# Attention and gated FFN on one core: the second half of the queries in four chunks of 256, and VectorE's second banks chosen by a budget

## The chip, the cores and the metric

The kernel runs on one NeuronCore of a Trainium2 chip. The metric is the device time in microseconds of one execution. Of the engines, TensorE (PE in the profile, its weight loads PEld) multiplies matrices into PSUM, ScalarE (ACT) evaluates exponentials and tanh, VectorE (DVE) does elementwise work, GpSimd (POOL) a few small operations, and SyncE (SP) issues nearly all transfers. Each engine works through its own instructions in order; an instruction that waits holds up all that stand behind it on its engine.

## What is computed

One layer in bf16: S = 2048 tokens, D = 512, H = 32 heads of 16, FFN width F = 1792. The gate is a plain sigmoid.

```python
qkv = (layernorm(x) @ wqkv).reshape(B, S, 3, H, 16)      # -> q, k, v of (B, H, S, 16)
p = softmax(einsum("bhqd,bhkd->bhqk", q, k) * 16 ** -0.5)
o = einsum("bhqk,bhkd->bhqd", p, v)                      # (B, H, S, 16)
h = x + o.transpose(0, 2, 1, 3).reshape(B, S, D) @ wo
n = layernorm(h)
out = h + (sigmoid(n @ w_gate) * (n @ w_up)) @ w_down
```

The scores are 32 x 2048 x 2048, so the kernel takes some 134 million exponentials; each row of scores has a bound subtracted beforehand (from the norms of q and k), so no maximum over scores is needed.

## The kernel before

**Chunks, units, steps.** The queries are cut into `CHUNKS` (L43): three of 512 columns and two of 256. Per chunk the 32 heads are worked in eight groups of four. A *unit* is one PSUM bank of 512 score columns: one head, one tile of 128 keys by 512 queries, or two key tiles by 256 queries (`per_bank`, L387). Three units are a *step* (`groups`, L394): their scores go to one of the two three-bank PSUM buffers `pss2`, and one ScalarE instruction (L782) takes the exponential of all three banks. There are 2048 units and so 683 steps; four steps are a *cycle* (`CYC`). 341 steps cover the first two chunks, 171 the third, 85 or 86 each of the last two.

**Second engine for exponentials.** In the steps in `split` (every fourth, L904) ScalarE takes two banks and VectorE the third, by five instructions that build the exponential from the bits of a float (`exp_bits`, `exp_first`, `exp_second`, `exp_third`, L800-L815) spread over this step and the next three. Before the change `twice` (L905-L911) marks further steps, every fourth or third cycle in fixed stretches, where another bank (a *second bank*) goes to VectorE. The first of a cycle is at step 0 of its four, the second at step 2. Their scratch lies in buffers that are free at the time (`scratch_of`, L793), for second banks in the one of the two `OT` buffers that is not in use.

**Scores.** `emit_scores` (L752) multiplies `KT` with `QB`. Heads lie so that two heads can share the array, each on 64 rows (*paired*, the shape 64*128 in the profile), or a head can use all 128 rows, half of them zero (*unpaired*, 128*128). Steps with an odd number are paired and even ones unpaired; in a cycle with a second bank all four are paired. `idle` (L756) holds when the filler has nothing for TensorE, and only in the first two steps of a cycle; such steps are unpaired in any case.

**PV and normalization.** `emit_pv` (L845) accumulates P times V (with a column of ones) over all keys in the one PSUM bank `acc`. At the end of a head group `emit_norm` (L822) copies `acc` to `xs_all` on VectorE (L826), sends the four rows of sums through DRAM to spread them, takes reciprocals (L837), sends them back as `rb_all` (L841) and scales into `OT` (L833): nine transfers on SP. The next group's queries come with four transfers of L221 and two of L231.

**Filler.** All other matmuls are put between the steps by a generator, `filler` (L730), driven by `emit_fill` (L867): projections of V, K and Q early on, then for each chunk `ffn_tasks` (L615): output projection with residual and layernorm (`ffn_wo`, or the denser `ffn_wo_tight` for the last chunks), gate and up (`ffn_up`), and down (`ffn_down`). `yield ("at", n)` means: go on at step n of a cycle. `ffn_up` gives a place to each gate block and each up block; a gate block is followed by tanh on ScalarE (L522), an up block by the multiply on VectorE (L530). A block fills one bank: one slice of 128 FFN columns by 512 queries (four matmuls), or two slices by 256 (eight). The list `(3, 1)` makes two blocks a cycle, `(3, 0, 1)` three (L582). All of filler shares one PSUM bank, "pm". An FFN starts at a step that depends on the end of its chunk's attention (L739) and after the FFN before it.

**Start and end.** The prologue (L236) makes what the first head group needs; its last V tiles are copied from PSUM to `Vaug` by ScalarE (`v_tile`, L307), between which the row with the bound is sent (`emit_q_bound`, L379, one of its two transfers issued by ScalarE). At the end `wo_early` (L626) does the last chunk's output projection of its first tile as far as it goes, and `ffn_last` (L641) the rest of the last chunk with nothing else beside it.

Of the kernel before, what the change touches and what calls it, by code (L numbers as in the profile page):

```python
# [13 lines left out]
ACT = mybir.ActivationFunctionType  # L14
AX = mybir.AxisListType


@with_exitstack
def kernel(
# [12 lines left out]
    P = 128  # L32
# [9 lines left out]
    TQ = QC // P  # L42
    CHUNKS = [(0, QC), (QC, QC), (2 * QC, QC), (3 * QC, QC // 2), (3 * QC + QC // 2, QC // 2)]  # L43
    NC = len(CHUNKS)
# [81 lines left out]
    o4 = 2 * GU * QC  # L126
    pt_late = slots(stg, 2) + [QTu[:, 0:3, 0:QC]]
    late_scratch = (stg[:, o4:o4 + 2 * QC].bitcast(mybir.dt.int32), e_man, y0[:].bitcast(FP32))
# [86 lines left out]
    def emit_q_rows(n):  # L215
        c, g = qgs[n]
        q0, w = CHUNKS[c]
        assert ("q", q0 // QC, g // 2) in ready
        for j in range(4):
            r = 64 * (g % 2) + DH * j  # L220
            nc.sync.dma_start(out=QB[n % 2][32 * j:32 * j + 32:2, j, 0:w],  # L221
                              in_=QTu[r:r + DH, g // 2, q0:q0 + w])

# [12 lines left out]
    def prologue(pro):  # L236
# [61 lines left out]
        def q_chunk():  # L298
            ps = pm_tile()
            for c in range(DC):  # L300
                qk_mm(ps, 0, 0, 0, c)
            nc.scalar.mul(out=QTu[:, 0, 0:QC], in_=ps[:], mul=QS)
            square("q", ps, QS)
            ready.add(("q", 0, 0))
            emit_q_rows(0)

        def v_tile(t):  # L307
            ps = pm_tile()
            for c in range(DC):
                v_mm(ps, t, c)  # L310
            v_store(t, ps, nc.scalar.copy)
            ready.add(("v", t))
# [133 lines left out]
    def fill_q0(b):  # L446
        ps = pm_tile()
        for c in range(DC):
            yield 1
            qk_mm(ps, 0, b, 0, c)  # L450
        q_store(QTu[:, b, 0:QC], ps)
        sq = squares(QTu[:, b, 0:QC])
        yield ("gap", 2)
        pn = pm_tile()
        yield 1
        norm_mm(pn, b, sq[:])
        q_root(pn, 0)
        q_bound(0, True)
        ready.add(("q", 0, b))
        ready.add(("b", 0, b))  # L460
        yield ("gap", 1)

    def fill_q(qc):
        cols = slice(qc * QC, (qc + 1) * QC)
        sq4 = stages[qc % 2]
        for b in range(4):
            ps = pm_tile()
            for c in range(DC):
                yield 1
                qk_mm(ps, 0, b, qc, c)  # L470
            q_store(QTu[:, b, cols], ps)
            nc.vector.tensor_tensor(out=sq4[:, b * QC:(b + 1) * QC], in0=QTu[:, b, cols], in1=QTu[:, b, cols],
                                    op=ALU.mult)
# [12 lines left out]

    def tiles_of(c):
        q0, w = CHUNKS[c]
        return range(q0 // P, (q0 + w) // P)

    def wo_mm(ps, c, tt, g):
        assert ("o", c, g) in ready
        nc.tensor.matmul(ps[:], lhsT=OT[c % 2][:, g, tt * P:(tt + 1) * P], rhs=wo_pad[:, g, :],  # L493
                         start=(g == 0), stop=(g == NG - 1))
# [129 lines left out]
    early = {}  # L624

    def wo_early(c):  # L626
# [14 lines left out]
    def ffn_last(c):  # L641
# [30 lines left out]
        nc.vector.tensor_tensor(out=OT[c % 2][:, NG - 1, 0:w], in0=xs, in1=rb[:, 0:w], op=ALU.mult)  # L672
        ready.add(("o", c, NG - 1))
        wo(1, 5, NG - 1)
        add_x(1)
# [54 lines left out]
    def filler():  # L730
# [91 lines left out]
    def emit_norm(c, g, i):  # L822
        w = CHUNKS[c][1]
        b = w // 32
        xs, rb, s32, r32 = (norm_part(t, w, g) for t in (xs_all, rb_all, s32_all, r32_all))
        nc.vector.tensor_copy(out=xs, in_=acc[:, 0:w])  # L826
        sd = dram.tile([4, w], FP32, name="sd", tag="sd%d" % w)
# [4 lines left out]
        def scale():  # L832
            nc.vector.tensor_tensor(out=OT[c % 2][:, g, 0:w], in0=xs, in1=rb, op=ALU.mult)  # L833
            ready.add(("o", c, g))
# [162 lines left out]
```

## Time and profile before

| | |
|---|---|
| median of 3 runs | 967.2 us (965.63 to 968.48) |
| profiled execution, its own time | 967.36 us |
| its span, first to last instruction | 965.6 us |
| first exponential starts, last one ends | 35.26, 934.89 us |
| granted TensorE clock, mean | 0.995 |
| transfers | 37500 packets, 28.38 MB |

The costliest groups of the page (instruction, tiles and shape, count, then busy time and mean of one, then the engine's idle time before them with what ended most of it):

```
L771 PE MATMUL pss<-QB,KT 64*128 64x512 bf16 (+3 forms) x2545 | 473.1, 338 | 86.8 <-ACT pt L782 40.5
L782 ACT ACTIVATE pt<-pss 128x1536 bf16<-128x1536 f32 (+1 forms) x392 | 500.6, 1361 | 18.0 <-PE pss L771 14.6
L801 DVE TENSOR_SCALAR stg<-pss 128x512 int32<-128x512 f32 x123 | 84.8, 690 | 73.0 <-PE pss L771 61.1
L852 PE MATMUL acc<-pt,Vaug 128*17 128x512 bf16 (+1 forms) x1471 | 114.1, 342 | 5.3 <-DVE xs_all L826 3.7
L533 PE MATMUL pm<-wd,reg 128*128 128x512 bf16 x173 | 51.5, 384 | 5.7 <-issue 3.2
```

The mean duration of a matmul is longer than its share of time, since matmuls overlap in the array. The exponentials appear in several groups, by the buffer that they write (pt, stg, wd, QTu); their counts add up to the 683 steps, so the n-th of them in time is step n, and a stage of the program can be placed in the trace by its steps.

### The profile page before, as it was taken

The numbers are of one execution on the slowest core, as the hardware profiler recorded it, in microseconds if no ns is written. First come the engines' busy times: TensorE is split into PE (matmuls) and PEld (weight loads), VectorE is DVE, ScalarE is ACT, GpSimd is POOL, SyncE is SP. The second block draws the span as 40 slices with busy tenths as digits, with TensorE's granted clock in tenths as the row PEclk, the third lists the DMA queues.
The fourth block names the chain that finished last, engine by engine and source line by source line (L and its number), as shares of the span: only waits on it lengthen the run. The fifth ranks groups of instructions, "written<-read, shape, count | busy, mean of one in ns | idle before, by whom it ended". The sixth has DMA issues, their size and how long they took to land.

```text
span 965.6 us, 17138 instructions
## 1 busy us (share of the span) xinstructions
PE 829.0 (86%) x6324; PEld 335.3 (35%) x6422; DVE 789.6 (82%) x1424; ACT 896.7 (93%) x769; POOL 39.0 (4%) x45
## 2 busy tenths in 40 slices
PE   4888888888888899888778999988788999998998
PEld 2221222222223232222223233222255545555646
DVE  8489999888878988898888888888899688777653
ACT  4799999999999999999999999989998999999872
POOL 4600000000000000000000000000000000000000
PEclk9999999999999999999999999999999999999999
DMA  5002341000013000000000000001011000110010
GB/s 161 20 1 56 114 95 38 15 15 3 15 25 104 15 15 16 9 19 27 15 26 27 16 16 15 9 20 26 16 26 27 16 10 16 27 32 16 9 35 12
DMA packets 37500, 28.38 MB, mean 29 GB/s; under 512 B 17708, under 2 KB 32776, under 8 KB 37416
## 3 DMA queue, kind: packets, MB, share of 16 engines
q1 hardware_dynamic: 35828, 25.71, 10.1%
q10 hardware_dynamic: 1588, 1.58, 0.5%
q8 instruction: 50, 0.82, 0.4%
q14 instruction: 34, 0.28, 0.1%
HBM read 20.31 MB, written 2.61 MB: 24 GB/s over the span
## 4 chain that ended last, share of the span: by engine, by line
PE 41%; DVE 26%; ACT 24%; issue 6%; DMA 2%; SPq 0%; ACTq 0%; DVEq 0%; POOL 0%; POOLq 0%
PE pss L771 20%; ACT pt L782 13%; PE acc L852 8%; PE pm L517 6%; ACT stg L782 4%; ACT wd L782 4%; DVE stg L801 3%; PE pm L533 2%; ACT QTu L782 2%; DVE st L137 2%; DVE reg L804 2%; PE pm L493 2%; DVE pt L814 2%; DVE y L810 1%; DVE reg L530 1%
## 5 line engine op out<-in xcount | busy, mean ns | idle before, releaser
L771 PE MATMUL pss<-QB,KT 64*128 64x512 bf16 (+3 forms) x2545 | 473.1, 338 | 86.8 <-ACT pt L782 40.5
L782 ACT ACTIVATE pt<-pss 128x1536 bf16<-128x1536 f32 (+1 forms) x392 | 500.6, 1361 | 18.0 <-PE pss L771 14.6
L771 PEld LDWEIGHTS <-KT 64*128 64x128 bf16 (+1 forms) x2560 | 179.0, 95 | 346.2 <-issue 237.4
L782 ACT ACTIVATE stg<-pss 128x1536 bf16<-128x1536 f32 (+1 forms) x140 | 183.3, 1358 | 5.0 <-PE pss L771 4.2
L801 DVE TENSOR_SCALAR stg<-pss 128x512 int32<-128x512 f32 x123 | 84.8, 690 | 73.0 <-PE pss L771 61.1
L852 PE MATMUL acc<-pt,Vaug 128*17 128x512 bf16 (+1 forms) x1471 | 114.1, 342 | 5.3 <-DVE xs_all L826 3.7
L782 ACT ACTIVATE wd<-pss 128x1536 bf16<-128x1536 f32 (+1 forms) x80 | 103.8, 1393 | 1.4 <-PE pss L771 1.3
L782 ACT ACTIVATE QTu<-pss 128x1024 bf16<-128x1024 f32 (+1 forms) x71 | 95.6, 1347 | 1.7 <-PE pss L771 1.2
L807 DVE SCALAR_TENSOR_TENSOR y<-reg 128x512 f32<-128x512 f32 x123 | 85.2, 693 | 4.2
L810 DVE SCALAR_TENSOR_TENSOR y<-y,reg 128x512 f32<-128x512 f32 x123 | 84.3, 685 | 1.1
L852 PEld LDWEIGHTS <-Vaug 128*17 128x17 bf16 x2560 | 50.5, 89 | 97.8 <-issue 83.2
L517 PE MATMUL pm<-reg,reg 128*128 128x512 bf16 (+1 forms) x252 | 55.6, 333 | 8.6 <-DVE reg L530 6.5
L517 PE MATMUL pm<-reg,wu 128*128 128x512 bf16 (+1 forms) x280 | 58.1, 338 | 1.5 <-ACT sg L522 1.2
L533 PE MATMUL pm<-wd,reg 128*128 128x512 bf16 x173 | 51.5, 384 | 5.7 <-issue 3.2
L804 DVE TENSOR_SCALAR reg<-stg 128x512 int32<-128x512 int32 x123 | 52.1, 423 | 2.0
L144 POOL TENSOR_TENSOR rs<-ve,pw_neg 128x1 f32<-128x1 f32 (+1 forms) x24 | 16.4, 685 | 896.0 <-DVE ve L142 895.8
L852 PE MATMUL acc<-stg,Vaug 128*17 128x256 bf16 (+1 forms) x564 | 50.7, 326 | 0.8 <-DVE stg L814 0.4
L530 DVE SCALAR_TENSOR_TENSOR reg<-sg,pm 128x512 bf16<-128x512 f32 x56 | 38.3, 683 | 14.5 <-PE pm L517 13.9
L814 DVE SCALAR_TENSOR_TENSOR pt<-y,stg 128x512 bf16<-128x512 f32 x70 | 47.9, 684 | 1.8
L522 ACT ACTIVATE sg<-pm 128x512 f32<-128x512 f32 x56 | 35.6, 636 | 10.0 <-PE pm L517 9.6
L801 DVE TENSOR_SCALAR wd<-pss 128x512 int32<-128x512 f32 x45 | 30.9, 687 | 14.0 <-PE pss L771 13.7
L163 PE MATMUL pm<-reg 128*128 128x512 bf16 x108 | 34.4, 391 | 2.9 <-issue 1.4
(121 smaller groups left out, 712.8 us busy)
## 6 DMA issues: line engine op xcount, KB each, us to landing
rb_all<-rd SPq DMA_DIRECT2D x96, 64.0 KB
reg<-in_A_x_dram SPq DMA_DIRECT2D x8, 256.0 KB
xr<-in_A_x_dram SPq DMA_DIRECT2D x16, 128.0 KB
out_dram<-ob SPq DMA_DIRECT2D x15, 128.0 KB
rb_all<-rd SPq DMA_DIRECT2D x60, 32.0 KB
KT<-stg SPq DMA_DIRECT2D x7, 256.0 KB
reg<-in_B_w_gate_dram SPq DMA_DIRECT2D x4, 448.0 KB
wu<-in_B_w_up_dram SPq DMA_DIRECT2D x4, 448.0 KB
```

Source lines behind the costliest of these rows:

```text
L517: nc.tensor.matmul(ps[:, i * w:(i + 1) * w], lhsT=wt[:, c, f * P:(f + 1) * P], rhs=hnT[:, c, 0:w], start=(c == 0), stop=(c == DC - 1))
L522: nc.scalar.activation(out=sg[:], in_=ps[:], func=ACT.Tanh, scale=0.5)
L530: nc.vector.scalar_tensor_tensor(out=out, in0=a, scalar=1.0, in1=b, op0=ALU.add, op1=ALU.mult)
L533: nc.tensor.matmul(ps[:], lhsT=hT[:, f, tt * P:(tt + 1) * P], rhs=wd[:, f, :], start=(f == 0), stop=(f == FC - 1))
L771: nc.tensor.matmul(pss[:, ui, h * w:(h + 1) * w], lhsT=KT[rows, g, kt * P:(kt + 1) * P], rhs=QB[n_qg % 2][rows, j, 0:w], start=True, stop= ...
L782: ex = nc.scalar.activation(out=pt[:, 0:na, :], in_=pss[:, 0:na, :], func=ACT.Exp, scale=DH ** -0.5 / QS)
L801: return nc.vector.tensor_scalar(out=e_bits, in0=src, scalar1=ONE_BITS, scalar2=0.0, op0=ALU.add, op1=ALU.max)
L804: nc.vector.tensor_scalar(out=e_man, in0=e_bits, scalar1=0x7FFFFF, scalar2=-0x40800000, op0=ALU.bitwise_and, op1=ALU.bitwise_or)
L807: nc.vector.scalar_tensor_tensor(out=e_pol, in0=m, scalar=PA, in1=m, op0=ALU.add, op1=ALU.mult)
L810: nc.vector.scalar_tensor_tensor(out=e_pol, in0=e_pol, scalar=PB, in1=e_man.bitcast(FP32), op0=ALU.add, op1=ALU.mult)
L814: nc.vector.scalar_tensor_tensor(out=dst, in0=e_pol, scalar=PC, in1=e_bits.bitcast(FP32), op0=ALU.add, op1=ALU.mult)
L852: nc.tensor.matmul(acc[32 * j:32 * j + VW, 0:w], lhsT=Vaug[:, kt, 4 * g + j, :], rhs=p[:, h * w:(h + 1) * w], start=(kt == 0), stop=(kt == ...
```

## The change

- `CHUNKS`: two chunks of 512 and four of 256. The third and fourth chunk cover together what the third did; there are six chunks, so eight more head groups.
- `ffn_up`: the places are `(3, 1)` for every chunk. The denser projection and down, and the earlier start of an FFN, go by the width of the chunk instead of its place from the end, so they hold for all chunks of 256.
- Second banks: in place of fixed lists, `plan_twice` runs at the start of each cycle from step 222 to 671. It adds to an account what VectorE has to spare in a cycle of the present phase of the filler (negative in the projection), and when the account is above 2.6 it draws 3.0 and marks this cycle. It marks 26 second banks in place of 23.
- Scratch of second banks: in `OT[0]` and the second 512 queries' part of `QTu`, whose layout changes so that 512 queries lie together. `OT` of a 256-wide chunk uses the first half of its buffer (`o_part`). The first group of the first 256-wide chunk puts its copy of `acc` in a part of `QTu`.
- `idle` holds for all steps of a cycle, so all its scores are unpaired. The two buffers of `pss2` change places.
- Start: the bound's row is sent before V tile 5 instead of tile 4, and V tiles 5 and 6 are copied by VectorE.
- End: the residual of the last chunk's first tile is added (an identity matmul) in `ffn_last` instead of `wo_early`, one projection matmul of its second tile moves ahead of the reciprocals' matmul, and `wo_early` goes on as soon as each head group is there.

```diff
-    CHUNKS = [(0, QC), (QC, QC), (2 * QC, QC), (3 * QC, QC // 2), (3 * QC + QC // 2, QC // 2)]
+    CHUNKS = [(0, QC), (QC, QC)] + [(q, QC // 2) for q in range(2 * QC, S, QC // 2)]
...
-    QTu = const.tile([P, 4, S], BF16)
+    QTu = const.tile([P, NQC, 4, QC], BF16)
...
         for t in range(3, NV0):
-            if t == 4:
+            if t == 5:
                 emit_q_bound(0, (nc.sync, nc.scalar))
-            v_tile(t)
+            v_tile(t, nc.scalar.copy if t < 5 else nc.vector.tensor_copy)
...
+    def o_part(c, g):
+        w = CHUNKS[c][1]
+        return OT[c % 2][:].rearrange("p g q -> p (g q)")[:, g * w:(g + 1) * w]
...
     def ffn_up(c):
         w = CHUNKS[c][1]
-        at = cycle((3, 1) if c + 2 < NC else (3, 0, 1))
+        at = cycle((3, 1))
...
     def ffn_tasks(c):
-        tight = c + 3 >= NC
+        tight = per_bank(c) > 1
         yield ("rate", 8.0)
+        phase[0] = "wo"
         yield from (ffn_wo_tight if tight else ffn_wo)(c)
+        phase[0] = "up"
         yield from ffn_up(c)
+        phase[0] = "down"
         yield from ffn_down(c, tight)
+        phase[0] = ""
...
         for g in range(NG - 1):
-            if g == NG - 2:
-                yield 1
-                nc.tensor.matmul(early[0][:], lhsT=ident_bf[:], rhs=early["x"][0][:], start=False, stop=False)
-                yield ("from", NS - 4)
+            while ("o", c, g) not in ready:
+                yield ("gap", 0)
             yield 1
             wo_mm(early[0], c, 0, g)
...
-        wo(1, 2, 5)
+        wo(1, 2, 6)
...
-        wo(1, 5, NG - 1)
+        wo(1, 6, NG - 1)
+        add_x(0)
         add_x(1)
...
-            yield ("from", int(first_step(c + 1)) + (11 if c + 3 >= NC else 15))
+            yield ("from", int(first_step(c + 1)) + (11 if per_bank(c) > 1 else 15))
...
     def emit_scores(i):
+        if i % CYC == 0:
+            plan_twice(i)
...
-        pss = pss2[i % 2]
-        idle = i >= 3 * FIRST and i % CYC < 2 and (state["done"] or state["wait"] > i + CYC)
+        pss = pss2[(i + 1) % 2]
+        idle = i >= 3 * FIRST and (state["done"] or state["wait"] > i + CYC)
...
         if i % CYC:
-            flat = OT[(int((i - 20) / SPC) + 1) % 2][:].rearrange("p g q -> p (g q)")
-            return (flat[:, 0:2 * QC].bitcast(mybir.dt.int32), flat[:, 2 * QC:4 * QC].bitcast(mybir.dt.int32),
-                    flat[:, 4 * QC:6 * QC].bitcast(FP32))
+            flat = OT[0][:].rearrange("p g q -> p (g q)")
+            q1 = QTu[:, 1].rearrange("p b q -> p (b q)")
+            parts = [flat[:, 0:2 * QC]] if i < 2 * SPC else [q1[:, 0:2 * QC]]
+            parts += [flat[:, 4 * QC:6 * QC], flat[:, 6 * QC:8 * QC]]
+            return tuple(t.bitcast(dt) for t, dt in zip(parts, (INT, INT, FP32)))
...
+        if g == 0 and c and CHUNKS[c - 1][1] > w:
+            xs = QTu[:, 0, 3, :].bitcast(FP32)
...
     split = set(range(8, G1, CYC))
     twice = set()
-    for qc in range(1, NQC):
-        n0 = int(qc * SPC) + 52
-        for n in range(n0, min(int((qc + 1) * SPC) + 16, int(first_step(NC - 1)) + 14)):
-            if n % ((4 if n < n0 + 56 else 3) * CYC) == 0:
-                twice.add(n + 2)
-    split |= twice
+    room = {"us": 0.0}
+
+    def plan_twice(n):
+        if n < int(SPC) + 52 or n >= G1 - 8:
+            return
+        free = {"wo": -0.8, "up": 0.9, "down": 0.85}.get(phase[0], 1.05)
+        room["us"] = max(0.0, room["us"] + free)
+        if room["us"] > 2.6:
+            room["us"] -= 2.6 + 0.4
+            twice.add(n + 2)
+            split.add(n + 2)
```

More of the change, by code (lines that the diff above doesn't have):

```diff
@@ L15 @@
 AX = mybir.AxisListType
+INT = mybir.dt.int32
 @with_exitstack
@@ L126 @@
     o4 = 2 * GU * QC
-    pt_late = slots(stg, 2) + [QTu[:, 0:3, 0:QC]]
+    pt_late = slots(stg, 2) + [QTu[:, 0, 0:3, :]]
     late_scratch = (stg[:, o4:o4 + 2 * QC].bitcast(mybir.dt.int32), e_man, y0[:].bitcast(FP32))
@@ L221, in emit_q_rows @@
             nc.sync.dma_start(out=QB[n % 2][32 * j:32 * j + 32:2, j, 0:w],
-                              in_=QTu[r:r + DH, g // 2, q0:q0 + w])
+                              in_=QTu[r:r + DH, q0 // QC, g // 2, q0 % QC:q0 % QC + w])
     def emit_q_bound(n, engs=(nc.sync, nc.sync)):
@@ L301, in q_chunk @@
                 qk_mm(ps, 0, 0, 0, c)
-            nc.scalar.mul(out=QTu[:, 0, 0:QC], in_=ps[:], mul=QS)
+            nc.scalar.mul(out=QTu[:, 0, 0, :], in_=ps[:], mul=QS)
             square("q", ps, QS)
@@ L305, in q_chunk, with v_tile @@
             emit_q_rows(0)
-        def v_tile(t):
+        def v_tile(t, copy=nc.scalar.copy):
             ps = pm_tile()
@@ L310, in v_tile @@
                 v_mm(ps, t, c)
-            v_store(t, ps, nc.scalar.copy)
+            v_store(t, ps, copy)
             ready.add(("v", t))
@@ L450, in fill_q0 @@
             qk_mm(ps, 0, b, 0, c)
-        q_store(QTu[:, b, 0:QC], ps)
-        sq = squares(QTu[:, b, 0:QC])
+        q_store(QTu[:, 0, b, :], ps)
+        sq = squares(QTu[:, 0, b, :])
         yield ("gap", 2)
@@ L463, in fill_q @@
     def fill_q(qc):
-        cols = slice(qc * QC, (qc + 1) * QC)
         sq4 = stages[qc % 2]
@@ L470, in fill_q @@
                 qk_mm(ps, 0, b, qc, c)
-            q_store(QTu[:, b, cols], ps)
-            nc.vector.tensor_tensor(out=sq4[:, b * QC:(b + 1) * QC], in0=QTu[:, b, cols], in1=QTu[:, b, cols],
+            q_store(QTu[:, qc, b, :], ps)
+            nc.vector.tensor_tensor(out=sq4[:, b * QC:(b + 1) * QC], in0=QTu[:, qc, b, :], in1=QTu[:, qc, b, :],
                                     op=ALU.mult)
@@ L489, in tiles_of @@
         return range(q0 // P, (q0 + w) // P)
+    def o_part(c, g):
+        w = CHUNKS[c][1]
+        return OT[c % 2][:].rearrange("p g q -> p (g q)")[:, g * w:(g + 1) * w]
     def wo_mm(ps, c, tt, g):
         assert ("o", c, g) in ready
-        nc.tensor.matmul(ps[:], lhsT=OT[c % 2][:, g, tt * P:(tt + 1) * P], rhs=wo_pad[:, g, :],
+        nc.tensor.matmul(ps[:], lhsT=o_part(c, g)[:, tt * P:(tt + 1) * P], rhs=wo_pad[:, g, :],
                          start=(g == 0), stop=(g == NG - 1))
@@ L624 @@
     early = {}
+    phase = [""]
     def wo_early(c):
@@ L671, in ffn_last @@
                              rhs=ident_f[:], start=True, stop=True)
-        nc.vector.tensor_tensor(out=OT[c % 2][:, NG - 1, 0:w], in0=xs, in1=rb[:, 0:w], op=ALU.mult)
+        nc.vector.tensor_tensor(out=o_part(c, NG - 1), in0=xs, in1=rb[:, 0:w], op=ALU.mult)
         ready.add(("o", c, NG - 1))
-        wo(1, 5, NG - 1)
+        wo(1, 6, NG - 1)
+        add_x(0)
         add_x(1)
@@ L832, in scale @@
         def scale():
-            nc.vector.tensor_tensor(out=OT[c % 2][:, g, 0:w], in0=xs, in1=rb, op=ALU.mult)
+            nc.vector.tensor_tensor(out=o_part(c, g), in0=xs, in1=rb, op=ALU.mult)
             ready.add(("o", c, g))
```

## The prediction

> **What bounds the kernel now.** I read the busy shares first, then the busy time by stretch, then the order of time inside three stretches.
>
> ```profile
> PE 829.0 (86%) x6324; PEld 335.3 (35%) x6422; DVE 789.6 (82%) x1424; ACT 896.7 (93%) x769; POOL 39.0 (4%) x45
> ...
> ACT  4799999999999999999999999989998999999872
> ```
>
> ScalarE is the busiest engine, nearly full from the third slice on, with dents from slice 27. Its work is the exponentials of line 782; their 683 instructions are the steps of the program. How long ScalarE needs for a step is read from starts, because its records overlap:
>
> ```profile
> 452.47 3.72 ACT L782 ACTIVATE pt<-pss 128x1536 bf16<-128x1536 f32 x3
> 456.03 2.42 ACT L782 ACTIVATE stg<-pss 128x1024 bf16<-128x1024 f32 x2
> 458.28 1.09 ACT L782 ACTIVATE QTu<-pss 128x1024 bf16<-128x1024 f32 x1
> ...
> 881.24 0.59 ACT L522 ACTIVATE sg<-pm 128x512 f32<-128x512 f32 x1
> 881.71 1.03 ACT L782 ACTIVATE stg<-pss 128x1024 bf16<-128x1024 f32 x1
> ```
>
> A three-bank step starts 1.330 us before the next (median over the trace), a two-bank one, whose third bank VectorE takes, 0.924, a tanh 0.477 (881.24 to 881.71). A cycle of four steps with one two-bank step thus needs 3 x 1.330 + 0.924 = 4.914 us of ScalarE, 0.406 less with a "second bank", 0.477 more with a tanh. What a stretch takes beyond that is **lost**. First exponential 35.26, last ends 934.89; after it 30.7 us of tail. The second half:
>
> ```profile
> 711.60:740.40 28.80, 24.92 (x280) 15.03 (x284) 25.65 (x54) 25.69 (x22) 2.35 (x4) 1.00 0.11 26
> 740.40:816.70 76.30, 71.31 (x774) 40.13 (x788) 61.13 (x110) 75.83 (x71) 0.00 (x0) 1.00 0.07 16
> 816.70:855.00 38.30, 35.70 (x389) 20.06 (x392) 29.25 (x54) 35.66 (x30) 0.00 (x0) 1.00 0.09 22
> ...
> 881.70:909.00 27.30, 24.99 (x288) 18.13 (x288) 18.02 (x32) 24.05 (x24) 0.00 (x0) 1.00 0.06 14
> 909.00:934.90 25.90, 23.67 (x271) 13.98 (x276) 16.02 (x30) 24.30 (x20) 0.00 (x0) 1.00 0.12 33
> ```
>
> (Columns: window, its length, busy PE, weight loads, VectorE, ScalarE.) Lost time, cycle by cycle, in us: steps 492-523 without FFN 1.3; output projection of the third chunk's four tiles (711.6-740.4) 4.2; its gate/up, two blocks a cycle, 1.7 in 14 cycles; its four down tiles 4.3; a gap 0.1; the fourth chunk's two projection tiles 1.4; its gate/up, three blocks a cycle (876-909), 5.0; its two down tiles 2.5. Sum 20.5. The largest rate is that of the three blocks:
>
> ```profile
> 881.88 1.03 PE L517 MATMUL pm<-reg,wu 128*128 128x256 bf16 x8 [0.45 <-ACT sg L522]
> ...
> 882.84 0.61 PE L771 MATMUL pss<-QB,KT 64*128 64x256 bf16 x6
> ...
> 883.55 1.45 ACT L782 ACTIVATE stg<-pss 128x1536 bf16<-128x1536 f32 x1 [0.81 <-PE pss L771]
> ...
> 884.05 1.03 PE L517 MATMUL pm<-reg,reg 128*128 128x256 bf16 x8 [0.60 <-DVE reg L530]
> ```
>
> There is one "pm" bank. TensorE, in order, waits until tanh or the multiply has emptied it, the scores behind wait too, and ScalarE idles 0.81 us.
>
> **The change, part by part.**
>
> *Three blocks become two.* All three FFNs of width 256 run gate/up as seven cycles. Two blocks a cycle cost 1.7 / 14 = 0.12 lost a cycle at 740-817. At half width a block is eight matmuls in 1.03-1.05 us; four full-width ones take 0.98 by the same timeline. So PE gains 2 x 0.07 on its 5.05 busy of 5.37: still below ScalarE. 21 cycles x 0.12 = 2.5, against 1.7 + 5.0.
>
> *Projection.* Three pairs of tiles at 1.4 = 4.2, against 4.2 + 1.4: a row of four tiles lets VectorE's backlog grow, a pair does not. *Down.* The six tiles remain; 6.6, against 4.3 + 2.5. *Idle steps* 492-523 are filled, since the third chunk is now done earlier: 0.3 with all gaps, against 1.4. Together 13.6 against 20.5: **-6.9**.
>
> *Second banks.* The budget, run through the program, chooses 26 in place of 23; from step 492 on 9 instead of 6, at 522, 538, 550, 582, 598, 610, 642, 658, 670. Each takes 0.406 from ScalarE and puts 690 + 423 + 693 + 685 + 684 ns = 3.17 us on VectorE. The trace gives the price: in gate/up at full width, cycles holding one lost 0.09 on the mean (plain ones -0.01) and the cycles behind them 0.39; in down 0.04 and 0.66. The next bank waits for VectorE, its score bank stays occupied, PE and then ScalarE wait. So one is worth nothing in an FFN. Three more: -1.2. The three in gate/up are in the 0.12 already; of six in down one is in the rate, five add about 0.64: +3.2. **+2.0**. Bounds: repaid in full -3.7 (9 x 0.406), or +6 if each also delays the emptying of pm:
>
> ```profile
> 838.10 0.68 DVE L538 SCALAR_TENSOR_TENSOR ob<-pm,reg 128x512 bf16<-128x512 f32 x1
> 838.84 0.81 PE L533 MATMUL pm<-wd,reg 128*128 128x512 bf16 x3 [0.99 <-DVE ob L538]
> ```
>
> *Chunk of 512 as two of 256.* Units, steps and exponentials stay (683). Scores and PV get 512 more matmuls each at half the columns: start to start 109 ns against 216, and the turn from one kind to the next costs 205 against 312, the same 96 more. There are eight more head-group ends, each with a copy of acc (422 ns), a reciprocal and a scale (416) on VectorE: 2.08 us for two against 1.62, +0.46 x 8 = 3.7 us, hidden under ScalarE where VectorE has room (16-18 of 20 us busy from 475 to 697). And 16 more transfers an end on SP (128 in all), which has them at this density from 697 us on and makes VectorE wait there only 2.6 (once, at the end) and 4.3 us (twice). What is not hidden: PV waits for the copy of acc, and the scores behind it. Seven such ends fall under the second chunk's FFN (steps 342-492); by cycles with and without one, 0 to 0.4 lost each, and 0.7 at worst in a projection. I take 0.15: **+1.0** (0 to +5).
>
> [...]
>
> *Unpaired scores in all idle steps.* Unpaired, three scores take 0.86 us, and behind a short step ScalarE waits 0.15-0.16 for them (1.08 in place of 0.92 at 458.28). Now the step behind a second bank waits too: two of them, **+0.3**.
>
> *Start.*
>
> ```profile
> 31.39 1.46 ACTq L231 DMA_DIRECT2D QB<-bnd  x1
> ...
> 32.89 1.57 ACT L210 CAST Vaug<-pm 128x512 bf16<-128x512 f32 x3 [2.36 <-PE pm L158]
> ...
> 34.55 1.02 PE L771 MATMUL pss<-QB,KT 64*128 64x512 bf16 x6 [2.06 <-ACT Vaug L210]
> ...
> 35.26 5.48 ACT L782 ACTIVATE pt<-pss 128x1536 bf16<-128x1536 f32 x4 [0.81 <-PE pss L771]
> ```
>
> ScalarE issues a transfer for 1.46 us with three V copies behind it; the first scores wait for the last copy. Now V tile 4 is copied before that issue and tiles 5 and 6 by VectorE (0.69 each, idle 5.27 us there). The first scores then need the bound's row, landed at 33.35 by the semaphore records, and the copy of tile 6, some 33.3: start 33.5, **-1.0** (0 to -1.2). ScalarE being full behind it, the shift reaches the end. The swapped order of the two score buffers costs nothing.
>
> *End.* The identity matmul of tile 0 moves from before the last PV (which waited up to 0.4 behind it and three projections) into the shadow of VectorE's scale; one more projection stands before the reciprocal's matmul (+0.1): **-0.1** (±0.4). Renamed layouts of QTu and OT and the new scratch cost nothing; they lie in storage whose readers are done.
>
> Sum: -6.9 + 2.0 + 1.0 + 0.3 - 1.0 - 0.1 = -4.7. The profiled execution took 967.36 (span 965.6 and 1.8 around it), 0.2 over the median of 967.2: 962.7 there, **962.5** against the median.
>
> **Rivals.** (a) *Given back.* Second banks in down cost +6 in place of +2, or the boundaries 4 in place of 1: 966.5 or 965.5. For it: pm and acc have one buffer each; against: the cycles of 697-817 hold as many ends and lose little. (b) *VectorE becomes the bound, slower.* The one mechanism is late emptying of acc and pm: a second bank (3.17 us) ahead of a copy in its queue. The worst cycle of that kind (838.84 above; ScalarE idle 1.15) lost 1.4. Six second banks in down at 1.4 instead of 0.64 add 4.6, seven ends at 0.7 instead of 0.15 add 3.9: 971. It decides once a late emptying costs more than some 1.1 us on the mean. Against: the measured mean is half that. (c) *More.* The five second banks in down lose nothing, because PE, which sets the pace there (5.1 of 5.3 us busy a cycle), pairs its scores in those cycles and is 0.23 us shorter: 3.2 less, 959.3. (d) *The budget does nothing:* three second banks neither way; inside the range of the forecast.
>
> **How the numbers follow.** Forecast 0.60 with its own range 959.5-965.5, (a) 0.16, (b) 0.11, (c) 0.13; (d) is within the first. 0.3% is 2.9 us, about what a measurement of this kernel tells from no change: faster means below 964.3. Of the forecast 0.49 lies below it and 0.11 above: faster 0.62, same 0.27, slower 0.11. Range 957.5 to 968: it holds all but (b). The range also has room for the clock: the granted TensorE clock falls to a half for 3.4 us three times (82, 266 and 649 us), in cycles that lost 1.4, 1.4 and 2.8; one such time more or fewer moves the sum by that.
>
> **What would show it.** First exponential near 34.2; no gate/up cycle above 6 us after 870; projection stretches in pairs losing under 2 us each; last exponential near 930; tail still 30.6. Wrong if cycles of the third and fourth chunk lose more than 0.3 on the mean in gate/up, if PE waits over some 8 us in all for the copies out of acc and pm, or if the first exponential has not moved.

## The result, and the profile after

The changed kernel is slower: 969.0 us (median of 16, 965.8 to 971.2) against 964.7 (16, 963.3 to 968.5), ratio 1.0038, 95% interval 1.0027 to 1.0050. The forecast was -4.7, which made 962.5 of the 967.2 that the kernel before had shown by then; measured is +4.3, which would make 971.5 of it, above the range of 957.5 to 968. Below, a "ratio" is always to the kernel before, run on the same chip, with its 95% interval in brackets, and "lost" is the time of a four-step cycle beyond what ScalarE needs, as in the prediction. In three of the experiments one execution took 1951 to 4309 us, and it is left out of the median.

The two profiled executions are nearly equal (967.21 after, 967.36 before; the first is at the low end of its kernel's runs), so their traces are compared for places, not for the sum. The busy shares of the changed kernel and ScalarE's row of slices:

```profile
PE 826.5 (86%) x7463; PEld 393.0 (41%) x7558; DVE 799.6 (83%) x1465; ACT 894.1 (93%) x767; POOL 38.9 (4%) x45
...
ACT  4799999999999999999999999999999899899972
```

VectorE has 10 us more and ScalarE 2.6 less; of the 2.6, the three additional second banks make 3 x 0.406 = 1.2. In ScalarE's row the dent of the three-block cycles is gone, and there are two at other places, 748 to 772 and 821 to 845 us. The start and the last FFN's gate/up by the timeline:

```profile
31.37 1.46 ACTq L232 DMA_DIRECT2D QB<-bnd  x1
...
33.47 1.02 PE L781 MATMUL pss<-QB,KT 64*128 64x512 bf16 x6 [0.99 <-DMA QB<-bnd]
...
34.23 1.45 ACT L792 ACTIVATE pt<-pss 128x1536 bf16<-128x1536 f32 x1 [2.86 <-PE pss L781]
...
882.14 0.59 ACT L526 ACTIVATE sg<-pm 128x512 f32<-128x512 f32 x1
882.62 5.20 ACT L792 ACTIVATE pt<-pss 128x1024 bf16<-128x1024 f32 x4
888.06 0.60 ACT L526 ACTIVATE sg<-pm 128x512 f32<-128x512 f32 x1 [0.24 <-PE pm L521]
```

The first exponential is at 34.23 in place of 35.26, and the scores now wait for the bound's row. From this tanh to the next is one cycle, 5.9 us with a wait of 0.24. It is the slowest of this gate/up (by its steps, 644 to 647, it took 6.16 us and lost 0.77); the others lost at most 0.22. Three stages by window (length, then busy PE, weight loads, VectorE, ScalarE):

```profile
754.00:780.00 26.00, 20.41 (x238) 12.52 (x238) 22.51 (x45) 23.56 (x20) 1.17 (x2) 1.00 0.12 30
780.00:834.00 54.00, 50.67 (x610) 33.09 (x613) 44.42 (x82) 52.16 (x47) 0.00 (x0) 1.00 0.06 16
...
860.00:900.00 40.00, 37.40 (x458) 25.63 (x458) 32.91 (x61) 39.61 (x38) 0.00 (x0) 1.00 0.07 15
```

Gate/up at 256 columns (the last two rows) runs at ScalarE's pace. Around a projection (first row) ScalarE idles 2.4 of 26 us, and VectorE is busy 22.5. Eleven cycles after step 341 lost more than 1 us. Eight of them come right behind a cycle with a second bank; the other three (from steps 504, 620 and 664) lose as much in the version without late second banks. The worst, the cycle from step 524, lost 1.93 us:

```profile
718.01 0.42 DVE L847 TENSOR_TENSOR OT<-xs_all,rb_all 128x256 bf16<-128x256 f32 x1
...
718.34 0.69 DVE L822 SCALAR_TENSOR_TENSOR OT<-OT 128x512 f32<-128x512 f32 x1
...
719.06 0.69 DVE L826 SCALAR_TENSOR_TENSOR stg<-OT,QTu 128x512 bf16<-128x512 f32 x1
...
720.73 0.68 DVE L534 SCALAR_TENSOR_TENSOR reg<-sg,pm 128x512 bf16<-128x512 f32 x1
721.33 0.41 DVE L840 COPY xs_all<-acc 128x256 f32<-128x256 f32 x1
...
721.80 0.40 PE L866 MATMUL acc<-stg,Vaug 128*17 128x256 bf16 x8 [1.74 <-DVE xs_all L840]
...
723.21 0.60 ACT L526 ACTIVATE sg<-pm 128x512 f32<-128x512 f32 x1 [1.36 <-PE pm L521]
```

The second bank was at step 522, four steps ahead of the end of a head group at 526. Its last two parts (718.34 and 719.06, which read `OT`, its scratch), the scale of an earlier group (718.01), the third bank's first parts and the FFN's multiply (720.73) all stand ahead of the copy of `acc` in VectorE's queue. PV of the next group waits 1.74 us for the copy, the gate block behind it is late, and ScalarE, in order, idles 1.36 us in tanh. In all, from 475 to 936 us (engine, what it waited for: sum, times, longest), after and then before:

```profile
PEld L781 <- DVE stg L813: 16.3, 26, 2.6
...
PE pss L781 <- DVE stg L813: 8.8, 9, 2.3
PE acc L866 <- DVE xs_all L840: 8.4, 12, 1.7
```

```profile
PEld L771 <- DVE stg L801: 13.4, 24, 1.3
...
PE pss L771 <- DVE stg L801: 3.5, 7, 0.8
...
PE acc L852 <- DVE xs_all L826: 2.5, 5, 1.0
```

TensorE waits three times as long for VectorE's copy out of `acc`, and two and a half times as long for the third bank's first part to release a score buffer.

### The profile page after: what moved, and what is told of

It reads as the page before. It is cut to its first block, busy times and chain, and to the rows that moved or that the text cites. A ratio compares the mean times of both kernels' runs of the same rounds, so it can differ in the third digit from the quotient of the medians.

```text
span 965.4 us, 19652 instructions
## 1 busy us (share of the span) xinstructions
PE 826.5 (86%) x7463; PEld 393.0 (41%) x7558; DVE 799.6 (83%) x1465; ACT 894.1 (93%) x767; POOL 38.9 (4%) x45
## 4 chain that ended last, share of the span: by engine, by line
PE 40%; DVE 28%; ACT 21%; issue 7%; DMA 2%; SPq 1%; DVEq 0%; ACTq 0%; POOL 0%; POOLq 0%
PE pss L781 20%; ACT pt L792 12%; PE acc L866 7%; PE pm L521 6%; ACT wd L792 4%; ACT stg L792 4%; DVE stg L813 3%; PE pm L537 2%; DVE pt L826 2%; DVE reg L816 2%; ACT QTu L792 2%; DVE st L138 2%; PE pm L497 2%; DVE y L822 2%; DVE OT L822 1%
## 5 line engine op out<-in xcount | busy, mean ns | idle before, releaser
L781 PE MATMUL pss<-QB,KT 64*128 64x256 bf16 (+3 forms) x3065 | 472.7, 309 | 84.5 <-ACT pt L792 38.6
L781 PEld LDWEIGHTS <-KT 64*128 64x128 bf16 (+1 forms) x3072 | 214.9, 95 | 317.9 <-issue 213.7
L866 PE MATMUL acc<-pt,Vaug 128*17 128x256 bf16 (+1 forms) x1762 | 113.2, 310 | 9.5 <-DVE xs_all L840 7.7
L866 PEld LDWEIGHTS <-Vaug 128*17 128x17 bf16 x3072 | 62.4, 89 | 90.7 <-issue 78.9
L521 PE MATMUL pm<-reg,reg 128*128 128x256 bf16 (+1 forms) x315 | 56.2, 305 | 5.7 <-DVE reg L534 4.0
L521 PE MATMUL pm<-reg,wu 128*128 128x256 bf16 (+1 forms) x336 | 58.3, 310 | 0.0
L526 ACT ACTIVATE sg<-pm 128x512 f32<-128x512 f32 x56 | 35.7, 638 | 11.3 <-PE pm L521 11.3
L521 PEld LDWEIGHTS <-reg 128*128 128x128 bf16 x336 | 29.3, 98 | 26.3 <-issue 17.0
```

The costliest lines, as they stand in the source:

```text
L521: nc.tensor.matmul(ps[:, i * w:(i + 1) * w], lhsT=wt[:, c, f * P:(f + 1) * P], rhs=hnT[:, c, 0:w], start=(c == 0), stop=(c == DC - 1))
L526: nc.scalar.activation(out=sg[:], in_=ps[:], func=ACT.Tanh, scale=0.5)
L781: nc.tensor.matmul(pss[:, ui, h * w:(h + 1) * w], lhsT=KT[rows, g, kt * P:(kt + 1) * P], rhs=QB[n_qg % 2][rows, j, 0:w], start=True, stop= ...
L866: nc.tensor.matmul(acc[32 * j:32 * j + VW, 0:w], lhsT=Vaug[:, kt, 4 * g + j, :], rhs=p[:, h * w:(h + 1) * w], start=(kt == 0), stop=(kt == ...
```

## The experiments

Times are medians in us.

**No second banks late** (in the changed kernel, none after step 341; 18 go, 8 stay).

```diff
-        if n < int(SPC) + 52 or n >= G1 - 8:
+        if n < int(SPC) + 52 or n >= 2 * int(SPC):
```

> The changed kernel without the second banks from step 341 on (18 of its 26 go; 8 stay). Theory V (VectorE is late: its second banks, the denser head-group ends and the waits for the sums' transfers meet in one in-order queue, so a second bank is not repaid): time at most 1 us above the changed kernel's 969.0 and perhaps up to 3 below, although ScalarE has 18 x 0.406 = 7.3 us more to do. Rival P (second banks are repaid, the loss is the chunks' own): 973 to 976.

956.9, ratio 0.9919 [0.9901, 0.9936]. The 18 second banks, which take 18 x 0.406 = 7.3 us from ScalarE, make the kernel some 12 us slower, four times what theory V allowed for. TensorE's waits for the copy out of `acc` (from 475 to 936 us) fall from 8.4 us in 12 times to 2.8 in 4. This version beats both kernels.

**The chunks with the old list** (changed kernel, but the old fixed list of 23 second banks, old idle rule, start and buffer order) and **the other way round** (old chunks with the budget, 24 second banks, and all small edits), which has the same lines with the signs changed.

```diff
-        if i % CYC == 0:
-            plan_twice(i)
...
+    for qc in range(1, NQC):
+        n0 = int(qc * SPC) + 52
+        for n in range(n0, min(int((qc + 1) * SPC) + 16, int(first_step(NC - 1)) + 14)):
+            if n % ((4 if n < n0 + 56 else 3) * CYC) == 0:
+                twice.add(n + 2)
+    split |= twice
```

> The changed kernel with the old fixed list of second banks (23), the old idle rule, the old start and the old order of the score buffers: the four chunks of 256 and two blocks a cycle alone (with the end that they need). Theory C (the chunks cost what the change costs: head-group ends and their transfers): 967 to 970. Rival B (the budget's placing, six in down, costs it): 960 to 964.

966.9, 1.0013 [0.9998, 1.0028]: with the old list the 256-wide chunks are still 10.0 above the version without late second banks, of which about 1 is for the small edits that it lacks (they are measured alone below).

> The kernel before with all of the change but the chunks: budget (24 second banks, up to step 611 as its scratch allows), idle rule, start, end, order of buffers. Theory C: 963 to 965, the start's 1 us less than before and a little back for the idle rule. Rival B: 966 to 970.

969.5, 1.0048 [1.0032, 1.0063]: the budget slows the old chunks too. The first of the two speaks for theory C, the second for rival B: with late second banks in place, each half of the change costs.

**The old idle rule** in the changed kernel.

```diff
-        idle = i >= 3 * FIRST and (state["done"] or state["wait"] > i + CYC)
+        idle = i >= 3 * FIRST and i % CYC < 2 and (state["done"] or state["wait"] > i + CYC)
```

> The changed kernel with the old idle rule (only the first two steps of a cycle unpaired). If the unpaired scores cost what cycles 328 to 347 show (some 0.2 us for each of five cycles): 0.5 to 1.3 below the changed kernel, 968. If half-clock times of TensorE follow from less paired work, their number falls or rises with it: the clock beside the times then differs from the changed kernel's.

970.4, 1.0054 [1.0038, 1.0071], against 1.0038 [1.0027, 1.0050] for the changed kernel: unpairing all idle steps costs nothing here; the direction is the opposite of what was forecast, but the intervals overlap.

**Where a second bank stands.** In the changed kernel, the same 12 head groups of twelve steps after step 398 get one second bank each: four steps ahead of the next group's end (the list below), four behind the last end (each late number 4 less), or on it (8 less). The eight early ones stay.

```diff
-            plan_twice(i)
...
+    twice |= set([234, 250, 262, 274, 290, 302, 318, 330, 406, 426, 438, 458, 470, 490, 522, 534, 586, 598, 650, 662])
```

> The changed kernel with 12 second banks after step 341 in place of the budget's 18, each four steps ahead of a 256-wide head-group end (the end's copy out of acc comes in the step behind the second bank's last part). Against the version without any second bank after step 341 (956.9) they take 12 x 0.406 = 4.9 us from ScalarE. Theory E (a second bank costs where its four VectorE instructions stand in front of the copy of acc of a head-group end): this is the worst place, 964 to 969. Rival L (the price is VectorE's load, wherever the bank stands): the same as the two other placements, all three within 1.5 us, near 956.9 + 12/18 of 12.1 = 965. Rival N (no price away from the budget's own places): near 952 to 955.

971.4, 1.0062 [1.0041, 1.0083].

> The same 12 head groups, each second bank four steps behind an end in place of four ahead of the next (in a head group of 12 steps). Theory E: the parts are done before the next copy of acc, so most of the 4.9 us stays: 953 to 958, at least 5 below the placement ahead of the ends. Rival L: the same as that one within 1.5 us.

961.9, 0.9964 [0.9946, 0.9983].

> The same 12 head groups, each second bank in the step of the end that opens them (eight steps earlier than ahead of the next end). Theory E: between the other two, 956 to 964, because the first part (690 ns) and the last two of the third bank before it stand ahead of the copy of acc but the rest behind. Rival L: as the others within 1.5 us.

959.1, 0.9930 [0.9912, 0.9949]. The same number of second banks differs by 12 us by place alone: rival L falls, and so does rival N. Theory E has the sign, but not all of the order: ahead is worse than its 964 to 969, behind is worse than its 953 to 958, and on the end, inside its 956 to 964, is best. By the traces, the cycles that hold the 12 ends behind the list's banks (steps 410 to 666) lose 1.64 us on the mean with the banks ahead, 0.20 behind, 0.35 on and 0.23 without any late bank; VectorE is busy 5.73, 4.30, 4.51 and 4.09 us in them, where ScalarE needs 4.91 (5.39 with a tanh). With the banks behind, the cycle ahead of the end's loses 0.82 instead. Taken over a bank's own cycle and the next, and against the same cycles without late banks, a second bank makes ScalarE lose 1.51 us ahead of an end, 0.77 behind it and 0.75 on it, where it saves 0.406. TensorE's wait for the copy, banks ahead and then on the ends:

```profile
PE acc L864 <- DVE xs_all L838: 18.1, 16, 1.8
...
DVE r_all L849 <- DMA s_all<-sd: 15.2, 9, 2.5
```

```profile
DVE r_all L849 <- DMA s_all<-sd: 5.8, 5, 2.3
...
PE acc L864 <- DVE xs_all L838: 4.1, 9, 1.0
```

Two lines differ, TensorE's wait for the copy and VectorE's wait, in its reciprocal, for the denominators. Even in the best place the 12 banks gain nothing against the 956.9 without them.

**No second bank at all.**

```diff
-        if i % CYC == 0:
-            plan_twice(i)
```

> The changed kernel without any second bank: the eight of the first half (steps 234 to 330, 512-wide head groups, no FFN beside them) go too. If those are worth what ScalarE saves (8 x 0.406 = 3.2): 960.2, against 956.9 with them. If they cost what the late ones cost on the mean (12.1 / 18 = 0.67 each): 951.5.

959.1, 0.9930 [0.9909, 0.9952]; with the eight early ones it was 0.9919 [0.9901, 0.9936]. By their profiled runs the eight lose 2.6 of the 3.2 us that they take from ScalarE (steps 200 to 340: 5.8 lost against 3.2). So they are worth about nothing, and cost nothing.

**The reciprocal later**, with the banks ahead of the ends and without late banks.

```diff
-            later(i + 10, scale)
-        later(i + 5, recip)
+            later(i + 10 + 2 * slow, scale)
+        slow = c >= 2 and c < NC - 1 and g < NG - 1
+        later(i + 5 + 2 * slow, recip)
```

> The version with 12 second banks ahead of the head-group ends (971.4), with the reciprocal two steps later behind the end (i + 7 in place of i + 5) and the scale at i + 12, for the 256-wide chunks but for the last chunk and each chunk's last head group. Theory D: what costs is that VectorE, in order, stands in the reciprocal waiting for the denominators' transfers (15.2 us in 9 waits there), with the third bank's parts behind it: 961 to 965. Rival K: what costs is the late copy out of acc itself (TensorE waits 18.1 us in 16 times for it): 968 to 973, and TensorE's waits for that copy stay near 18.

970.6, 1.0053 [1.0032, 1.0074]: theory D falls; VectorE's wait in the reciprocal is down to 2.3 us in 2 times, and the time has not moved. It isn't what K expected either: TensorE's waits for the copy are 12.9 us in 14 times, not near 18. The loss has moved: the cycles of the 12 ends lose 1.02 in place of 1.64, the ones ahead of them 0.71 in place of 0.26.

> The version without second banks after step 341 (956.9) with the same later reciprocal and scale. If VectorE's waits for the denominators (13.5 us in 10 times in its profiled run) reach the end in part: 953 to 956. If they are hidden under ScalarE: 956 to 958.

961.8, 0.9965 [0.9953, 0.9978], outside both expectations. The wait went to the scale, which now has only three steps for the second round of transfers; at 666 us:

```profile
665.79 0.43 DVE L847 TENSOR_TENSOR OT<-xs_all,rb_all 128x256 bf16<-128x256 f32 x1 [4.60 <-DMA rb_all<-rd]
...
669.87 1.45 ACT L792 ACTIVATE pt<-pss 128x1536 bf16<-128x1536 f32 x1 [2.99 <-PE pss L781]
```

So the comparison of the two with the later reciprocal is not clean; what it shows is that this edit mends nothing.

**Before without its late second banks** and **the small edits alone**, both on the kernel before.

```diff
-            if n % ((4 if n < n0 + 56 else 3) * CYC) == 0:
+            if n % ((4 if n < n0 + 56 else 3) * CYC) == 0 and n + 2 < int(2 * SPC):
```

> The kernel before, without its 14 second banks after step 341. Theory E has fewer head-group ends there (24 in place of 32 after step 341) and the fixed list meets them less often, but the price is of the same kind: 957 to 962, so that the kernel before paid for its second banks too. Rival: the price came with the 256-wide ends alone; then the 14 were worth 14 x 0.406 = 5.7 and it is 968 to 971.

966.7, 1.0016 [1.0001, 1.0030], between the two expectations: before, 14 late second banks were worth 2.0 (0.1 to 2.9 by the interval) of the 5.7 us that they take from ScalarE.

The small edits (with the change's edits at the end):

```diff
-        pss = pss2[i % 2]
-        idle = i >= 3 * FIRST and i % CYC < 2 and (state["done"] or state["wait"] > i + CYC)
+        pss = pss2[(i + 1) % 2]
+        idle = i >= 3 * FIRST and (state["done"] or state["wait"] > i + CYC)
...
-            if t == 4:
+            if t == 5:
                 emit_q_bound(0, (nc.sync, nc.scalar))
-            v_tile(t)
+            v_tile(t, nc.scalar.copy if t < 5 else nc.vector.tensor_copy)
```

> The kernel before with the small edits alone: V copies and the bound's issue at the start, unpaired scores in all idle steps, the order of the two score buffers, and the end. The old fixed list of second banks and the old chunks stay. As predicted for these parts (-1.0 + 0.3 - 0.1 = -0.8): 962.5 to 965, and then the budget is what made the version without the chunk change 5 us slower. Rival: the small edits cost: 967 to 970.

963.6, 0.9990 [0.9977, 1.0003]: -1.1, where -0.8 was forecast; the interval still holds no change. Against it the version without the chunk change, which has the budget besides, is 5.8 slower: the budget's places cost that much even between the wider head groups.

**Acc in two halves**: groups of 256 columns alternate between the halves of the one bank.

```diff
+    def acc_part(c, g):
+        w = CHUNKS[c][1]
+        o = w * (g % 2) if w < QC else 0
+        return acc[:, o:o + w]
-        nc.vector.tensor_copy(out=xs, in_=acc[:, 0:w])
+        nc.vector.tensor_copy(out=xs, in_=acc_part(c, g))
...
-                nc.tensor.matmul(acc[32 * j:32 * j + VW, 0:w], lhsT=Vaug[:, kt, 4 * g + j, :],
+                nc.tensor.matmul(acc_part(c, g)[32 * j:32 * j + VW, :], lhsT=Vaug[:, kt, 4 * g + j, :],
```

> The changed kernel, with the sums of P V of a 256-wide head group in alternate halves of the acc bank, so that the next group's first matmuls need not wait for VectorE's copy of the last one. Theory K (the late copy out of acc holds TensorE, the scores behind it and ScalarE): most of the price of the 18 second banks goes, TensorE's waits for that copy fall from 8.4 us to under 2, and the time falls from 969.0 to 954 to 962. Rival Q (the price is VectorE's queue itself: the next third bank's first part comes late, which keeps its score bank, whoever holds acc): 965 to 969, the waits for score banks and for pm stay.

970.6, 1.0065 [1.0050, 1.0080].

> The version with 12 second banks ahead of the head-group ends (971.4), with the same alternate halves. Theory K: 954 to 961, below the 959.1 of the banks on the ends. Rival Q: 966 to 971.

971.5, 1.0077 [1.0065, 1.0089].

> The version without second banks after step 341 (956.9), with the same alternate halves. Its waits of TensorE for the copy are 2.8 us in 4 times: 955 to 957 by both theories; below the other two if second banks are worth nothing even then (rival Q), above them by up to 4 if they are worth what ScalarE saves (theory K).

957.2, 0.9929 [0.9915, 0.9943]. The first two are just above rival Q's numbers, but they do not speak against K, since the wait is still there (banks ahead, two halves):

```profile
PE acc L869 <- DVE xs_all L843: 17.4, 15, 1.7
```

The program still makes TensorE's write to the bank wait for VectorE's read of it, whichever half: 17.4 us in 15 times, where it was 18.1 in 16 without the halves. No run here tried the halves without that wait.

**The copy by ScalarE at the 12 ends**, with the banks ahead of them and, as control, without late banks.

```diff
+    BY_ACT = [410, 430, 442, 462, 474, 494, 526, 538, 590, 602, 654, 666]
-        nc.vector.tensor_copy(out=xs, in_=acc[:, 0:w])
+        (nc.scalar.copy if i in BY_ACT else nc.vector.tensor_copy)(out=xs, in_=acc[:, 0:w])
```

> The version with 12 second banks ahead of the head-group ends (971.4), where ScalarE in place of VectorE copies acc at those 12 ends (ScalarE isn't late, so TensorE's wait for the copy goes; it costs ScalarE some 0.45 us each by VectorE's 0.42 for the copy, 5.4 in all). Theory K (the late copy): at most 3 above the same edit without second banks (its own control, expected near 962), so 957 to 965. Rival Q (VectorE's queue itself, the next third bank's first part): 8 us or more above the control, 970 to 976.

966.0, 1.0010 [0.9998, 1.0021].

> The control: the version without second banks after step 341 (956.9) with the same 12 copies by ScalarE. ScalarE takes 12 x 0.45 = 5.4 us more and sets the pace: 959 to 963 by both theories.

968.0, 1.0037 [1.0025, 1.0050]: the control itself is 11 above the version without the edit, 0.92 for each copy of 0.395 us, more than expected, for a reason that stays open. Beside this control the 12 banks ahead of the ends gain 2.0 where they had cost some 14. The sign is K's, and the level is not a clean measure: with the banks ahead, TensorE waits for ScalarE's copies too (9.5 us in 10 times). By cycles, those that hold the 12 ends lose 0.98 in place of 1.64 (a copy delays ScalarE's next step by 0.25 us, which is counted as needed), about half of what they lose above the 0.23 without a bank. That this half is due to the copy's place in VectorE's queue is likely but not shown: VectorE also has 0.4 us less to do in these cycles, and for the control no such figure is at hand.

**The third bank dropped** in the cycle of each of the 12 ends, the second bank ahead of it left.

```diff
+    split |= twice
+    split -= set([408, 428, 440, 460, 472, 492, 524, 536, 588, 600, 652, 664])
```

> The version with 12 second banks ahead of the ends (971.4), where the third bank of the cycle that holds each of those 12 ends stays with ScalarE. VectorE and ScalarE have the same work in sum as in the version without second banks after step 341 (956.9), moved by some steps. If the price is VectorE's work in the cycle of the end (3.17 us of the third bank beside the rest of the second and the end's 1.04): 955 to 960. If a second bank costs by itself, wherever VectorE stands: 965 or more.

958.5, 0.9938 [0.9924, 0.9953]. VectorE is now busy 2.97 us in those cycles and they lose 0.14. The price is gone, with every second bank where it was: it is not the second bank as such. VectorE has as many banks here as without late ones, so this run alone can't tell its work in one cycle from its work in sum; the three placements above do, with 12 us between equal sums.

## Why the prediction was wrong, step by step

**The step that failed** is "second banks ... +2.0", with its ground: "so one is worth nothing in an FFN", the price read as a mean of 0.39 + 0.09 in gate/up and 0.04 + 0.66 in down. The runs put the late second banks at +11.8 us after (4.3 above the kernel before with them, 7.4 below without) where before they were worth 2.0: a swing of +13.8. The mean was about right for where it was taken, and did not carry over. With the list of places unchanged, late second banks gain 2.0 with the old chunks and cost about 8.9 with the new ones (966.9 against 956.9, less the 1.1 of the small edits), so most of the swing comes with the chunks and the rest with the budget's places.

Part of it is where a bank meets the end of a head group. Of the 14 late second banks before, one lies four steps ahead of a head-group end; of the 18 after, six do, because ends come every 8 or 12 steps where the third chunk had one each 20 or 24. The cycle behind one of these six lost 1.21 us on the mean in the changed kernel, and 1.64 where all 12 were put there. The kernel before had shown this: behind its one such bank (step 470, end at 474) TensorE waited 0.96 us for the copy, and the cycle from step 472 lost 2.84, the most of all behind a second bank. The prediction listed this cycle with the half-clock times, as chance. The working priced the ends (0.15) and the second banks as two sums; they meet in one cycle, where 3.17 us of the third bank, the rest of the second, the end's copy, reciprocal and scale and the FFN's multiplies make 5.7 us for VectorE against ScalarE's 4.91 to 5.39. The budget counts what VectorE has to spare by phase of the filler and does not know of the ends.

The six are the dearest, but they do not carry the whole price. By the traces of the changed kernel and of the version without late banks, the 18 banks' cycles and those behind them lose 17.3 us more with the banks: 7.5 at the six ahead of an end (1.25 each), 6.4 at the seven on an end (0.9 each) and 3.5 at the five that lie eight steps ahead (0.7 each). So in each of the three groups a late bank costs more, on the mean, than the 0.406 that it saves; VectorE's fuller queue is the likely cause there too, but no run takes it apart for these twelve. The sum also had no term for the nine late banks before step 492, which the budget moved: steps 344 to 491 lost 11.3 us where 8.8 before and 1.0 for the ends were reckoned, and steps 492 to 679 lost 20.7 where the prediction's terms make 17.1 (20.5 - 6.9 + 3.2 + 0.3).

**The rival with 0.11** had the mechanism and the point: a late emptying of `acc`, which "decides once a late emptying costs more than some 1.1 us on the mean"; the mean is 1.21 behind the six and 1.64 behind the twelve put there, though only 0.90 behind all 18. It also took its price, 1.4, from a cycle of this kind, and then set it aside because "the measured mean is half that". It names the emptying alone; by the copies on ScalarE that is some half of it at the 12 ends, and VectorE's whole queue in that cycle is the rest. That its 971 comes so near the measured difference is in part luck: 3.9 of its 8.5 us were for ends without any second bank, and the cycles of such ends lose only 0.23.

**The chunks: right, and worth more.** Forecast were -6.9 for denser and evener FFNs and +1.0 for the ends. Without late second banks on either side, changed and old kernel stand at -7.4 and +2.0 against the kernel before; with the small edits' -1.1 taken off, the chunks alone are worth -8.3 where -5.9 was forecast. In the profiled run steps 644 to 663, where the three blocks had been, lost 1.4 in place of 5.0, and the projections in pairs lost 1.9, 1.7 and 1.9, under the 2 named. The 1024 additional weight loads (512 for scores, 94 to 97 ns each on the mean, and 512 for PV, 89 ns, in the changed kernel's trace) show nowhere as time: PEld went from 335 to 393 us busy while PE went from 829.0 to 826.5, and the version without late banks is the fastest.

**The small edits: right.** Start -1.0 (34.23); with the idle rule and the end -1.1 together, forecast -0.8. The idle rule's own +0.3 has not shown.

The three parts, -1.1 - 8.3 + 13.8, give back the measured +4.3 because each is a difference of the same medians; their sum confirms nothing. Of the signs named beforehand, four spoke against the forecast: the last exponential (it ended at 935.1, not near 930), TensorE's waits for the copies out of `acc` and "pm" (8.4 us for `acc` alone), one cycle above 6 us in the gate/up after 870 (6.16), and the gate/up of the third chunk (steps 512 to 539), which lost 0.46 on the mean, while that of the fourth (572 to 599) lost 0.06. The first exponential, the tail (30.3) and the projections came as forecast.

**The clock.** The range left room for one stretch at half clock more or fewer, as chance. It may partly be a consequence: the mean granted clock over the 16 runs of the changed kernel is 0.9950, against 0.9956 to 0.9984 (some 0.997) for the kernel before in the runs beside the experiments, and within these 16 runs the time falls by about 6.5 us for 0.01 of clock. That makes 0.4 to 2.2 us of the 4.3, an estimate from these numbers; that the late VectorE is what lowers the clock is seen only in single places (last section).

## What to carry to other kernels

A price for moving work to a second engine, read as a mean, holds only for the places where it was read: before carrying it over, list which other work of that engine falls into the same cycle at the new places, and compare its sum with the pace of the bound engine cycle by cycle, not over a stage. A budget that decides where extra work goes has to count the periodic work of that engine (here the head-group ends) and not only the phase; that such a budget would gain is not shown, since even the best of the three placements did not. Here the helper engine was 83% busy, and removing a part of its help was the gain: with 18 of 26 second banks taken away the kernel is 0.8% faster than before.

## What the runs showed of the hardware

In these traces a stretch of 3.4 us with TensorE busy 0.50 or less was followed by half clock in 20 of 21 cases (the count is below). The version with the banks ahead of the ends, two such pairs by window (columns as above; the last but two is the granted clock):

```profile
588.20:591.60 3.40, 1.67 (x34) 0.88 (x31) 3.33 (x7) 3.14 (x3) 0.00 (x0) 1.00 0.01 3
591.60:595.00 3.40, 3.07 (x19) 1.47 (x14) 1.01 (x2) 0.60 (x1) 0.00 (x0) 0.50 0.02 2
676.90:680.30 3.40, 1.64 (x22) 0.94 (x22) 3.33 (x7) 2.33 (x2) 0.00 (x0) 1.00 0.12 39
680.30:683.70 3.40, 3.19 (x29) 1.76 (x32) 3.16 (x7) 3.09 (x3) 0.00 (x0) 0.51 0.17 40
```

VectorE is busy 3.33 of 3.40 us, TensorE 1.67, because it waits for the copy of `acc` (it is idle 1.73 us of the first stretch, and the longest such wait of this execution after 475 us is 1.8), and then TensorE does the late work at a granted clock of 0.50 and ScalarE has 0.60 us of work in 3.4 (3.09 in the second pair). So a late VectorE is paid twice in the first pair. All 44 half-clock stretches (granted clock 0.50; 3.413 us each in the trace before, 6.827 in the changed kernel's one from 81.6 us) between the first and the last exponential, in 19 profiled executions, began behind 3.4 us with TensorE busy 0.65 or less; within an execution they start a multiple of 3.413 us apart. Of the stretches of that grid in the same time, 21 had TensorE busy 0.50 or less, and 20 of them were followed by half clock (the changed kernel's 719.9 to 723.3, 0.49 busy, was not); of the 105 with 0.50 to 0.65, 24 were.
